# A parallel attention and MLP kernel on one core: x of the second parity and the attention output transposed on VectorE and moved by transfers instead of on TensorE

## The chip, the core and the metric

One core of one Trainium2 chip. The metric is the device time of one execution in microseconds (us); lower is better. The kernel before took 1194.18 us (median of 3 runs, 1194.16 to 1194.31).

## The reference, cut to what matters

```python
x = A_x                                   # 1 x 2048 x 576, float32
xn = _layernorm(x, axis=-1)
return x + _A_ref(xn, A_wqkv, A_wo) + _B_ref(xn, B_w1, B_w2)

def _A_ref(x, wqkv, wo):                  # 32 heads of 18, window 8, dilation 2
    q, k, v = (x @ wqkv) split in three and in heads
    # row s looks at rows s, s-2, ..., s-14; those before row 0 are masked
    o = softmax(q . k_window * 18**-0.5) @ v_window
    return o @ wo

def _B_ref(x, w1, w2):                    # Dff = 4608
    return relu(x @ w1) @ w2
```

## The kernel before, in words

**Tiles and parities.** Because the dilation is 2, even rows attend only to even rows and odd rows to odd rows. The kernel handles one parity ("phase", `ph`) after the other. A phase has 1024 rows, as eight tiles `X[ph, i]` of 128 partitions by 576 columns; partition p of tile i holds row 8p + i of its parity, so a window of 8 rows lies along the free axis.

**Split products.** Each float32 operand is cut into a rounded part (`hi`, float32r) and a rest (`lo`), and a product is made of three terms: hi.hi, lo.hi and hi.lo. The 576 rows of the contraction are four blocks of 128 and a remainder of 64; the fifth block holds the remainder twice, as hi in partitions 0 to 63 and as lo in 64 to 127 (`mix`). `TERMS` lists the 14 matmuls of one product.

**Transposes.** TensorE contracts over partitions, so the normalised x (`xn`) and the attention output must be turned, columns into partitions. `transpose_split` (L264) does this with five TensorE transposes of 128x128 into PSUM (L273, L274). ScalarE then copies `hi` out of PSUM (L276) and `mix` (L278), and VectorE makes `lo` (L277) and the second half of `mix` (L279). `make_xt` (L283) does it for x; two tiles share one `xT` buffer of 256 columns. `wo_a` (L407) does it for the attention output, and `wo_b` (L416) multiplies with `wo` in 28 matmuls of 288 columns and adds the result to `X`. `norm` (L252) copies the last 64 columns once more beside themselves (L261), and `wo_a` does the same into `od` (L411), for the doubled fifth block.

**The steps.** The main loop (L547) runs over 288 steps, 144 per phase: 12 chunks of three 128-wide slices of Dff, by four blocks `tb` of 256 rows, by the three slices. Step n issues `h_mm` of step n + 2 (14 matmuls of 256 columns, the first product of the MLP), then whatever `at` put at this step, then `o_mm` of step n (12 matmuls of 288 columns), then what `late` put there, then VectorE work of the attention from a list (`run_bg`). `h_mm` ends with a ScalarE relu (L447, `hhi`) and a VectorE rest (L448, `hlo`); it has two PSUM buffers, and so has `o_mm`, whose sums VectorE adds to `X` after three steps (L471). Nothing is reordered afterwards: each engine executes its instructions in the order in which the Python code emits them, and an instruction that waits holds up all that stands behind it on its engine.

**What stands where.** In each phase, steps 7 to 95 (counted within the phase) hold the projections for q, k, v of four groups of eight heads; steps 123 to 131 hold `wo_a` and `wo_b` of the eight tiles, one tile per step, `wo_a` at the end of step 123 + i and `wo_b` in the step after it. In the first phase, the x tiles of the second parity are prepared from step 129 on, one every two steps: `load_x`, `stats`, `norm` and `make_xt` (L511 to L515). Block tb of the second phase is first needed by `h_mm` in step 142 + 3 tb.

**Transfers.** All loads and stores are issued by SyncE (SP), in order: three per w1 slice, one per w2 slice, five or six per group of wqkv and of wo, one per x tile and per output tile. A load waits for its staging buffer (`stp`, four of them) to be free. In the built program the transfers of SP and ScalarE use eight semaphores in turn, so each transfer also waits until the eighth before it has landed. ScalarE issues the halo copies of k and v (L318), from SBUF to SBUF.

Of the kernel before, what the change touches and what calls it, by code (L numbers as in the profile page):

```python
# [10 lines left out]
F32 = mybir.dt.float32  # L11
F32R = mybir.dt.float32r
AF = mybir.ActivationFunctionType
ALU = mybir.AluOpType
# [3 lines left out]
P = 128  # L18
# [9 lines left out]
EPS = 1e-5  # L28

UNIT0, UNIT_STEP, WO_AT = 7, 27, 8  # L30
HEADW = (-5, -2, -1, 0, 0, 1)

HEAD = (
# [22 lines left out]
def tile_body(ctx: ExitStack, tc: tile.TileContext, x, wqkv, wo, w1, w2, out):  # L56
    nc = tc.nc
    S, D = x.shape
# [5 lines left out]
    KT = 4  # L64
    DR = D - KT * P
    D2 = D // 2
# [4 lines left out]
    ctx.enter_context(tc.manual_schedule())  # L71
    pool = lambda name, bufs, **k: ctx.enter_context(tc.tile_pool(name=name, bufs=bufs, **k))
    consts = pool("consts", 1)
    xp = pool("xp", 12)
    xtp = pool("xtp", NTB)
    qop = pool("qop", 1)
    kp = pool("kp", 1)
# [9 lines left out]
    tmp = pool("tmp", 2)  # L87
# [4 lines left out]
    f32 = lambda ap: ap.bitcast(F32)  # L92
# [18 lines left out]
    def mm(o, l, r, start, stop, n):  # L111
        nc.tensor.matmul(o, l, r, start=start, stop=stop)  # L112
        t["pe"] += n / 2400.0 + 0.002

    def dve(n):
        t["dve"] += (n + 130) / 960.0
# [112 lines left out]
    X, XT, XN, MR = {}, {}, {}, {}  # L229
# [21 lines left out]

    def norm(ph, i, act=False):  # L252
        nm, r = MR.pop((ph, i))
        xn = tmp.tile([P, 640], F32, name="xn")
        if act:
            nc.scalar.activation(xn[:, 0:D], X[ph, i], AF.Identity, bias=nm)  # L256
            nc.scalar.activation(xn[:, 0:D], xn[:, 0:D], AF.Copy, scale=r)  # L257
        else:
            nc.vector.tensor_scalar(xn[:, 0:D], X[ph, i], nm, r, op0=ALU.add, op1=ALU.mult)
            dve(600)  # L260
        nc.scalar.activation(xn[:, D:640], xn[:, KT * P : D], AF.Copy)  # L261
        XN[ph, i] = xn

    def transpose_split(src, last, hi, mix, lo, free=False):  # L264

        if free:
            pa, pb = (ps_o.tile([P, 2, 512], F32, name="po")[:, 0, :] for _ in range(2))
            pa, pb = pa.rearrange("p (k c) -> p k c", k=KT), pb[:, 0:P]
        else:
            pa = ps_m.tile([P, KT, P], F32, name="pm")  # L270
            pb = ps_m.tile([P, P], F32, name="pm")
        for k in range(KT):
            nc.tensor.transpose(pa[:, k, :], src[:, k * P : (k + 1) * P], ident)  # L273
        nc.tensor.transpose(pb, last, ident)  # L274
        t["pe"] += 5 * 0.06
        nc.scalar.activation(hi, pa, AF.Copy)  # L276
        nc.vector.tensor_tensor(lo, pa, f32(hi), op=ALU.subtract)  # L277
        nc.scalar.activation(mix, pb, AF.Copy)  # L278
        nc.vector.tensor_tensor(mix[DR:P], pb[DR:P], f32(mix[DR:P]), op=ALU.subtract)  # L279
        dve(512)  # L280
        dve(128)

    def make_xt(ph, i, free=False):  # L283
        tb, h = divmod(i, 2)
        if h == 0:
            XT[ph, tb] = xtp.tile([P, 9, TBN], F32R, name="xT")
        d = XT[ph, tb][:, :, h * P : (h + 1) * P]
        xn = XN.pop((ph, i))
        transpose_split(xn[:, 0:512], xn[:, 512:640], d[:, 0:4, :], d[:, 4, :], d[:, 5:9, :], free)


    TERMS = [(k, k) for k in range(KT)] + [(5 + k, k) for k in range(KT)] + [(4, 4)] + [(k, 5 + k) for k in range(5)]


    QO, KK, VV = {}, {}, {}
# [109 lines left out]
    OT = {}  # L405

    def wo_a(ph, i):  # L407
        assert (ph, i) in ready, (ph, i, len(bg))
        o = QO[ph][:, i, :]
        od = tmp.tile([P, 2, DR], F32, name="od")  # L410
        nc.scalar.activation(od, o[:, None, KT * P : D].to_broadcast([P, 2, DR]), AF.Copy)  # L411
        d = tmp.tile([P, 9, P], F32R, name="oT", bufs=1)
        transpose_split(o[:, 0:512], od.rearrange("p a b -> p (a b)"), d[:, 0:4, :], d[:, 4, :], d[:, 5:9, :])
        OT[ph, i] = d

    def wo_b(ph, i):  # L416
        d, w = OT.pop((ph, i)), WO[ph]
        po = [ps_m.tile([P, D2], F32, name="pm") for _ in range(2)]
        for j, (a, b) in enumerate(TERMS):
            for h in range(2):  # L420
                mm(po[h], d[:, a, :], w[b][:, h * D2 : (h + 1) * D2], j == 0, j == len(TERMS) - 1, D2)
        for h in range(2):
            acc = X[ph, i][:, h * D2 : (h + 1) * D2]
            nc.vector.tensor_tensor(acc, po[h], acc, op=ALU.add)
            dve(D2)
# [53 lines left out]
    def at(n, f, *a):  # L479
        todo.setdefault(n, []).append((f, a))  # L480
# [3 lines left out]
    def late(n, f, *a):  # L484
        todo_late.setdefault(n, []).append((f, a))

    plan = []
    for ph in range(NPH):
        b = ph * SPP
        for c in range(NCH):  # L490
            for f in range(C):
                s = b + c * SPC + f
                first = ph == c == 0
                plan.append((HEADW[f] if first else s - 5, w1_task, ((ph, c, f), c * C + f)))
                plan.append((HEADW[3 + f] if first else s - 3, w2_task, ((ph, c, f), c * C + f)))
        for u in range(NU):
            s = b + UNIT0 + u * UNIT_STEP
            plan.append((s - 5, wq_tasks, ((ph, u), u)))
            for i in range(NI):
                at(s + i, qkv_tile, ph, u, i)  # L500
            late(s + NI + 1, attention, ph, u)
        s = b + UNIT0 + NU * UNIT_STEP + WO_AT
        plan.append((s - 8, wo_tasks, (ph,)))
        for i in range(NI):
            late(s + i, wo_a, ph, i)
            at(s + i + 1, wo_b, ph, i)
            at(s + i + 1, done, ph, i)
        if ph + 1 < NPH:
            e = b + SPP - SPC
            for i in range(NI):  # L510
                z = e + 3 + 2 * i  # L511
                at(z - 6, load_x, ph + 1, i)
                late(z - 2, stats, ph + 1, i)
                late(z - 1, norm, ph + 1, i)
                at(z + 1, make_xt, ph + 1, i)  # L515
    for step, f, a in sorted(plan, key=lambda z: z[0]):
        if f in (wq_tasks, wo_tasks):
            f([step + k for k in range(5)], *a)
# [13 lines left out]
    held = []  # L532
    run_splits(-5)
    norm(0, 0)
    norm(0, 1)
    stats(0, 2)
    make_xt(0, 0)
    make_xt(0, 1, True)
    for f in held:
        f()  # L540
# [45 lines left out]
```

## Time and profile before

| | before |
|---|---|
| median of 3 runs | 1194.18 us |
| profiled execution: its time | 1194.74 us |
| profiled execution: its span in the trace | 1193.0 us |
| granted TensorE clock, mean | 0.998 |
| VectorE busy | 812.5 us (68% of the span), 1269 instructions |
| ScalarE busy | 310.5 us (26%), 790 instructions |
| GpSimd busy | 40.1 us (3%) |
| transfers | 84883 packets, 75.67 MB; SP's queue 19.7% of 16 DMA engines |

How to read the profile: it shows one execution. PE is TensorE's matmuls and PEld its weight loads, DVE is VectorE, ACT is ScalarE, POOL is GpSimd, SPq and ACTq are the issuing of transfers by SP and ScalarE. L112 is line 112, the helper through which all matmuls go, so groups of it are told apart by their tiles: `ph` for `h_mm`, `po` for `o_mm`, `pm<-wq,xT` for the projections, `pm<-wq,oT` and `pm<-v,oT` for `wo_b`. "128x576 f32 x192 | 143.9, 757" reads: 192 instructions on 128 partitions by 576 columns, 143.9 us in sum, 757 ns in the mean. In a timeline the first number is the start in us from the beginning of the span, the second the duration of the merged group of xN instructions. PE durations overlap, since matmuls are pipelined; the distance from one start to the next is what counts.

### The profile page before, as it was taken

What the parts mean: (1) busy time and instruction counts of PE and PEld (TensorE: products, weight loads), DVE (VectorE), ACT (ScalarE), POOL (GpSimd) and SP (SyncE); (2) the same over time, 40 slices, a digit from 0 to 9 for tenths busy, and PEclk for the clock granted to TensorE, in tenths of its full rate; (3) what the DMA queues carried; (4) which work ended last, traced back from release to release, by engine and by line L of the source; (5) the groups of instructions that cost most, each with busy time, mean ns of one, the idle gap of its engine ahead of it and who ended that gap; (6) DMA issues with size and microseconds to landing.
All of it is one profiled execution on the core that took longest, in us unless ns stands there. A gap on an engine that the chain in (4) does not pass through costs nothing.

```text
span 1193.0 us, 21739 instructions
## 1 busy us (share of the span) xinstructions
PE 1183.8 (99%) x9016; PEld 1172.8 (98%) x9016; DVE 812.5 (68%) x1269; ACT 310.5 (26%) x790; POOL 40.1 (3%) x63
## 2 busy tenths in 40 slices
PE   8999999999999999999999999999999999999998
PEld 7999999999999999999999999999999999999998
DVE  7516875888687578875573278858767875886732
ACT  5422222131222222322233123122221322222210
POOL 2000000010000000000120000000100000000000
PEclk9999999999999999999999999999999999999999
DMA  5312122130321311402242113031302312212002
GB/s 172 84 32 82 42 76 55 38 107 1 98 58 44 86 33 43 114 11 73 91 130 74 46 54 90 22 85 29 86 21 79 83 38 79 63 42 73 21 1 80
DMA packets 84883, 75.67 MB, mean 63 GB/s; under 512 B 6592, under 2 KB 68288, under 8 KB 84784
## 3 DMA queue, kind: packets, MB, share of 16 engines
q1 hardware_dynamic: 82256, 66.08, 19.7%
q10 hardware_dynamic: 2528, 8.20, 2.4%
q8 instruction: 71, 1.16, 0.4%
q14 instruction: 28, 0.23, 0.1%
HBM read 61.34 MB, written 4.72 MB: 55 GB/s over the span
## 4 chain that ended last, share of the span: by engine, by line
PE 98%; DVE 1%; SPq 0%; ACT 0%; DMA 0%; issue 0%; DVEq 0%; ACTq 0%
PE ph L112 39%; PE po L112 38%; PE pm L112 20%; PE pm L273 1%; PE pm L274 0%; DMA st<-in_w 0%; SPq L235 0%; DVE pr L380 0%; DVE pr L373 0%; SPq L157 0%; SPq L162 0%; SPq L161 0%; PE po L273 0%; ACT xn L257 0%; ACT xn L256 0%
## 5 line engine op out<-in xcount | busy, mean ns | idle before, releaser
L112 PE MATMUL ph<-xT,w1t 128*128 128x256 f32 x4032 | 514.2, 279 | 1.3 <-ACT xT L276 0.6
L112 PEld LDWEIGHTS ph<-xT,w1t 128*128 128x128 f32 x4032 | 491.6, 188 | 2.0 <-ACT xT L276 0.8
L112 PE MATMUL po<-w2t,hhi 128*128 128x288 f32 x2304 | 400.5, 296 | 0.4 <-DVE w2t L143 0.3
L112 PEld LDWEIGHTS po<-w2t,hhi 128*128 128x128 f32 x2304 | 337.0, 188 | 2.0 <-DVE w2t L143 0.5
L447 ACT ACTIVATE hhi<-ph 128x256 fp32r<-128x256 f32 x288 | 110.2, 382 | 531.8 <-PE ph L112 512.5
L112 PE MATMUL po<-w2t,hlo 128*128 128x288 f32 x1152 | 244.7, 293 | 0.0
L448 DVE SCALAR_TENSOR_TENSOR hlo<-ph,hhi 128x256 fp32r<-128x256 f32 x288 | 121.7, 423 | 169.1 <-ACT hhi L447 167.8
L471 DVE TENSOR_TENSOR x<-po,x 128x576 f32<-128x576 f32 x192 | 143.9, 757 | 69.8 <-PE po L112 66.3
L112 PE MATMUL pm<-wq,xT 128*128 128x432 f32 x896 | 185.5, 358 | 0.0
L112 PEld LDWEIGHTS po<-w2t,hlo 128*128 128x128 f32 x1152 | 183.7, 188 | 0.0
L112 PEld LDWEIGHTS pm<-wq,xT 128*128 128x128 f32 x896 | 163.8, 188 | 5.6
L343 DVE TENSOR_TENSOR pr<-qo,k 128x1152 f32<-128x1152 f32 x64 | 85.9, 1349 | 0.0
L373 DVE TENSOR_TENSOR pr<-lg,v 128x1152 f32<-128x1152 f32 x64 | 85.0, 1352 | 0.3
L346 DVE TENSOR_REDUCE lg<-pr 128x64 f32<-128x1152 f32 x64 | 85.0, 1343 | 0.0
L143 DVE TENSOR_TENSOR w2t<-st,w2t 128x576 fp32r<-128x576 f32 x72 | 54.3, 755 | 45.0 <-ACT w2t L146 44.7
L380 DVE TENSOR_TENSOR pr<-pr 128x288 f32<-128x288 f32 (+1 forms) x128 | 70.5, 602 | 0.1
L143 DVE TENSOR_TENSOR w1t<-st,w1t 128x640 fp32r<-128x640 f32 x72 | 59.0, 820 | 15.0 <-ACT w1t L146 14.8
L146 ACT ACTIVATE w2t<-st 128x576 fp32r<-128x576 f32 x72 | 49.1, 684 | 45.0 <-PE po L112 31.0
L146 ACT ACTIVATE w1t<-st 128x640 fp32r<-128x640 f32 x72 | 53.0, 737 | 13.2 <-DMA st<-in_w 13.2
L312 ACT ACTIVATE k<-pm 128x144 f32<-128x144 f32 x64 | 18.7, 292 | 142.8 <-PE pm L112 142.6
L112 PE MATMUL pm<-wq,oT 128*128 128x288 f32 x352 | 51.7, 299 | 0.0
L112 PEld LDWEIGHTS pm<-wq,oT 128*128 128x128 f32 x352 | 47.9, 188 | 1.7
(63 smaller groups left out, 398.0 us busy)
## 6 DMA issues: line engine op xcount, KB each, us to landing
st<-in_w SPq DMA_DIRECT2D x72, 288.0 KB, 3.0
st<-in_w SPq DMA_DIRECT2D x72, 256.0 KB, 3.0
st<-in_wqkv SPq DMA_DIRECT2D x32, 216.0 KB, 3.0
st<-in_w SPq DMA_DIRECT2D x144, 32.0 KB, 2.7
out<-x SPq DMA_DIRECT2D x16, 288.0 KB, 2.1
x<-in_x SPq DMA_DIRECT2D x15, 288.0 KB, 3.9
k<-k ACTq DMA_DIRECT2D x8, 441.0 KB, 3.9
v<-v ACTq DMA_DIRECT2D x8, 441.0 KB, 4.6
```

The costliest lines, as they stand in the source:

```text
L112: nc.tensor.matmul(o, l, r, start=start, stop=stop)
L143: nc.vector.tensor_tensor(lo, src, f32(hi), op=ALU.subtract)
L146: nc.scalar.activation(hi, src, AF.Copy)
L273: nc.tensor.transpose(pa[:, k, :], src[:, k * P : (k + 1) * P], ident)
L312: nc.scalar.activation(k[:, W - 1 + i, :], pq[:, 1, :], AF.Copy)
L343: nc.vector.tensor_tensor(pr[i], q, window(k, i), op=ALU.mult)
L346: nc.vector.tensor_reduce(lg[:, i], pr.pop(i).rearrange(heads, d=Dh), axis=AX.X, op=ALU.add)
L373: nc.vector.tensor_tensor(pr[i].rearrange(heads, d=Dh), e, window(v, i).rearrange(heads, d=Dh), op=ALU.mult)
L380: nc.vector.tensor_tensor(o, z[:, 0:n], z[:, n : 2 * n], op=ALU.add)
L447: nc.scalar.activation(hi, pt, AF.Relu)
L448: nc.vector.scalar_tensor_tensor(lo, pt, 0.0, f32(hi), op0=ALU.max, op1=ALU.subtract)
L471: nc.vector.tensor_tensor(acc, PO[k][:, :, 0:D2], acc, op=ALU.add)
```

## The change

The tiles of the first parity are treated as before. For the eight x tiles of the second parity and the sixteen attention-output tiles, the five TensorE transposes go. Instead `blocks` turns each 32x32 block in place with two VectorE transposes (576 columns, and the last 64 once more) into a tile `tr`, and then SP issues 16 transfers from SBUF to SBUF, each of 32 partitions by 5 runs of 32 columns (128 bytes a run, 20 KB in all), which put block (a, b) where block (b, a) belongs. `split` then makes `hi`, `mix` and `lo` from SBUF; for the attention output `lo` overwrites the turned tile.

The plan moves with it. `wo_a` now stands at steps 123 + (0, 1, 3, 4, 6, 7, 9, 10), the split `wo_s` two steps later at the step's end, and `wo_b` three steps later. For x tile i of the second parity, with z = 134 + 2i: from i = 2 on the load is issued in step z - 2, `stats`, `norm` and the turn all stand at the end of step z, and `make_xt` (the split) at the end of step z + 2, ahead of the `stats` of tile i + 1. There are ten buffers for x tiles instead of twelve, so tile i of the second parity, for i from 2 on, takes the buffer of tile i - 2 of the first and waits for its store. `xn` gets three buffers, which the turned attention output shares. The copy of the last 64 columns (L261, L411) goes where `blocks` is used.

```diff
-    xp = pool("xp", 12)
+    xp = pool("xp", 10)
...
+    def blocks(src, dst):
+        tr = tmp.tile([P, 5, P], F32, name="tr")
+        flat = tr.rearrange("p k c -> p (k c)")
+        nc.vector.transpose(flat[:, 0:D], src)
+        nc.vector.transpose(flat[:, D:640], src[:, KT * P : D])
...
+        for a in range(4):
+            rows = slice(32 * a, 32 * a + 32)
+            for b in range(4):
+                nc.sync.dma_start(dst[32 * b : 32 * b + 32, :, rows], tr[rows, :, 32 * b : 32 * b + 32])
+
+    def turn_x(ph, i):
+        xn = XN[ph, i]
+        blocks(xn[:, 0:D], xn.rearrange("p (k c) -> p k c", c=P))
+
+    def split(z, hi, mix, lo):
+        nc.scalar.activation(hi, z[:, 0:KT], AF.Copy)
+        nc.scalar.activation(mix, z[:, KT], AF.Copy)
+        nc.vector.tensor_tensor(lo, z[:, 0:KT], f32(hi), op=ALU.subtract)
+        nc.vector.tensor_tensor(mix[DR:P], z[DR:P, KT], f32(mix[DR:P]), op=ALU.subtract)
...
+        if ph:
+            split(xn.rearrange("p (k c) -> p k c", c=P), d[:, 0:4, :], d[:, 4, :], d[:, 5:9, :])
+            return
         transpose_split(xn[:, 0:512], xn[:, 512:640], d[:, 0:4, :], d[:, 4, :], d[:, 5:9, :], free)
...
-        transpose_split(o[:, 0:512], od.rearrange("p a b -> p (a b)"), d[:, 0:4, :], d[:, 4, :], d[:, 5:9, :])
-        OT[ph, i] = d
+        OT[ph, i] = tmp.tile([P, 5, P], F32R, name="xn", bufs=3)
+        blocks(QO[ph][:, i, :], f32(OT[ph, i]))
+
+    def wo_s(ph, i):
+        z = OT[ph, i]
+        d = tmp.tile([P, 5, P], F32R, name="oT", bufs=1)
+        split(f32(z), d[:, 0:4], d[:, 4], z[:, 0:4])
...
-            late(s + i, wo_a, ph, i)
-            at(s + i + 1, wo_b, ph, i)
+            z = s + WO_STEPS[i]
+            late(z, wo_a, ph, i)
+            late(z + 2, wo_s, ph, i)
+            at(z + 3, wo_b, ph, i)
...
-                z = e + 3 + 2 * i
-                at(z - 6, load_x, ph + 1, i)
-                late(z - 2, stats, ph + 1, i)
-                late(z - 1, norm, ph + 1, i)
-                at(z + 1, make_xt, ph + 1, i)
+                z = e + 2 + 2 * i
+                at(z - 2 if i > 1 else z - 6, load_x, ph + 1, i)
+                late(z - 2 if i < 2 else z, stats, ph + 1, i)
+                late(z - 1 if i < 2 else z, norm, ph + 1, i)
+                late(z if i < 2 else z, turn_x, ph + 1, i)
+                late(z + 2, make_xt, ph + 1, i)
```

More of the change, by code (lines that the diff above doesn't have):

```diff
@@ L30 @@
 UNIT0, UNIT_STEP, WO_AT = 7, 27, 8
+WO_STEPS = (0, 1, 3, 4, 6, 7, 9, 10)
 HEADW = (-5, -2, -1, 0, 0, 1)
@@ L253, in norm @@
         nm, r = MR.pop((ph, i))
-        xn = tmp.tile([P, 640], F32, name="xn")
+        xn = tmp.tile([P, 640], F32, name="xn", bufs=3)
         if act:
@@ L260, in norm @@
             dve(600)
-        nc.scalar.activation(xn[:, D:640], xn[:, KT * P : D], AF.Copy)
+        if ph == 0:
+            nc.scalar.activation(xn[:, D:640], xn[:, KT * P : D], AF.Copy)
         XN[ph, i] = xn
+    def blocks(src, dst):
[3 more added lines that the diff above has]
+        nc.vector.transpose(flat[:, D:640], src[:, KT * P : D])
+        dve(D)
+        dve(DR)
+        for a in range(4):
[10 more added lines that the diff above has]
+        nc.vector.tensor_tensor(mix[DR:P], z[DR:P, KT], f32(mix[DR:P]), op=ALU.subtract)
+        dve(512)
+        dve(128)
     def transpose_split(src, last, hi, mix, lo, free=False):
@@ L408, in wo_a @@
         assert (ph, i) in ready, (ph, i, len(bg))
[L409 to L412, printed above, removed]
-        transpose_split(o[:, 0:512], od.rearrange("p a b -> p (a b)"), d[:, 0:4, :], d[:, 4, :], d[:, 5:9, :])
-        OT[ph, i] = d
+        OT[ph, i] = tmp.tile([P, 5, P], F32R, name="xn", bufs=3)
[4 more added lines that the diff above has]
+        split(f32(z), d[:, 0:4], d[:, 4], z[:, 0:4])
+        OT[ph, i] = [d[:, k] for k in range(5)] + [z[:, k] for k in range(4)]
     def wo_b(ph, i):
@@ L420, in wo_b @@
             for h in range(2):
-                mm(po[h], d[:, a, :], w[b][:, h * D2 : (h + 1) * D2], j == 0, j == len(TERMS) - 1, D2)
+                mm(po[h], d[a], w[b][:, h * D2 : (h + 1) * D2], j == 0, j == len(TERMS) - 1, D2)
         for h in range(2):
@@ L504, in tile_body @@
         for i in range(NI):
-            late(s + i, wo_a, ph, i)
-            at(s + i + 1, wo_b, ph, i)
-            at(s + i + 1, done, ph, i)
+            z = s + WO_STEPS[i]
+            late(z, wo_a, ph, i)
+            late(z + 2, wo_s, ph, i)
+            at(z + 3, wo_b, ph, i)
+            at(z + 3, done, ph, i)
         if ph + 1 < NPH:
```

## Prediction

> **What bounds the kernel now.** I read the page's busy line and chain first, then PE's timeline for what one step costs, then SP's timeline and the rows of single lines for what one transfer costs.
>
> ```profile
> PE 1183.8 (99%) x9016; PEld 1172.8 (98%) x9016; DVE 812.5 (68%) x1269; ACT 310.5 (26%) x790; POOL 40.1 (3%) x63
> ...
> PE 98%; DVE 1%; SPq 0%; ACT 0%; DMA 0%; issue 0%; DVEq 0%; ACTq 0%
> ```
>
> TensorE bounds everything; nothing waits long ahead of it. So whatever leaves TensorE is gained whole, and whatever delays it is lost whole. PE's timeline around one `wo_b`, and around plain steps later on:
>
> ```profile
> 504.25 0.49 PEld L273 LDWEIGHTS pm<-ident,qo 128*128 128x128 f32 x4
> 504.71 0.14 PEld L274 LDWEIGHTS pm<-ident,od 128*128 128x128 f32 x1
> 504.82 1.68 PEld L112 LDWEIGHTS ph<-xT,w1t 128*128 128x128 f32 x14
> 504.84 1.85 PE L112 MATMUL ph<-xT,w1t 128*128 128x256 f32 x14
> 506.53 3.24 PE L112 MATMUL pm<-wq,oT 128*128 128x288 f32 x22
> 510.40 0.69 PE L112 MATMUL po<-w2t,hhi 128*128 128x288 f32 x4
> 512.45 1.85 PE L112 MATMUL ph<-xT,w1t 128*128 128x256 f32 x14
> ```
> ```profile
> 616.80 1.78 PE L112 MATMUL ph<-xT,w1t 128*128 128x256 f32 x14
> 618.42 0.69 PE L112 MATMUL po<-w2t,hhi 128*128 128x288 f32 x4
> 620.00 1.78 PE L112 MATMUL ph<-xT,w1t 128*128 128x256 f32 x14
> ```
>
> A plain step is 620.00 - 616.80 = 3.2 us: 1.6 for `h_mm`, 1.6 for `o_mm`. A step with `wo_b` and transposes is 512.45 - 504.84 = 7.6; five transposes hold the array from 504.25 to 504.82, 0.57 us; so `wo_b` adds 7.6 - 0.57 - 3.2 = 3.84.
>
> **What goes.** 24 tiles lose five transposes each: 24 x 0.57 = **13.7 us gained** on the bounding engine. The copies of the last 64 columns go from ScalarE, which is idle most of the time: nothing.
>
> **What comes, per tile.** Two VectorE transposes, 16 SP transfers, two ScalarE and two VectorE instructions of the split. The question is how long one tile takes from its turn to its split, and who stands behind it. First the issuing on SP:
>
> ```profile
> 2.11 0.43 SPq L157 DMA_DIRECT2D st<-in_w  x1
> 2.59 0.55 SPq L161 DMA_DIRECT2D st<-in_w  x1
> ...
> 8.42 2.01 SPq L235 DMA_DIRECT2D x<-in_x  x4
> ```
> ```profile
> L173 SPq DMA_DIRECT2D st<-in_w x72: 327/347/530, 10.6 to 1126.4; - x72
> ```
> ```profile
> L161 SPq DMA_DIRECT2D st<-in_w x72: 506/510/1649, 2.6 to 1080.8; - x72
> ```
> ```profile
> L318 ACTq DMA_DIRECT2D v<-v x16: 562/830/834, 91.2 to 1004.4; - x16
> ```
>
> From 2.11 to 8.42 us SP issues eleven transfers in a row, (8.42 - 2.11) / 11 = 0.574 each; L161, which always follows another at once, takes 0.51 and a gap of 0.05 (2.59 - 2.11 - 0.43). No row shows 32 partitions by 5 runs. Below it stands the lone L173, 0.35 + 0.05 = 0.40; above it ScalarE's back-to-back SBUF copies, 0.83 + 0.05 = 0.88. I take **0.575**, the row of a long run on the same queue. Sixteen take 9.2 us, and the last is issued 8.6 after the first. Then the landing, and the data itself:
>
> ```profile
> st<-in_w SPq DMA_DIRECT2D x144, 32.0 KB, 2.7
> out<-x SPq DMA_DIRECT2D x16, 288.0 KB, 2.1
> ...
> v<-v ACTq DMA_DIRECT2D x8, 441.0 KB, 4.6
> ...
> v<-v ACTq DMA_DIRECT2D x8, 59.1 KB, 4.0
> ```
> ```profile
> 656.00:661.00 5.00, 5.00 (x34) 4.90 (x33) 1.73 (x4) 1.04 (x4) 0.00 (x0) 1.00 0.23 66
> ```
>
> I take 2.7 from issue to landing, the nearest size (32 KB; the new ones have 20), between 2.1 and 4.0. So a tile lands 8.6 + 2.7 = 11.3 us after its first issue. The wait for the eighth transfer before costs nothing until landing takes 8 x 0.575 = 4.6. The window holds one w1 slice, 640 packets of 512 bytes and 48 for semaphores: 0.23 x 5 x 16 / 688 = 26.7 ns of one engine each. A tile has 16 x 176 = 2816 packets, at most 2816 x 26.7 ns / 16 = 4.7 us on 16 engines, less than the 9.2 of issuing.
>
> The Trainium skill ("DMA: Bandwidth & Descriptors", Issuing engines are not separate DMA queues) says that the sequencer's time to initiate a transfer is usually small relative to the transfer itself. Under that rule the packets set the pace, which is the third rival below; the L161 row, 0.51 us of issue for 32 KB, speaks against it.
>
> ```profile
> L146 ACT ACTIVATE w2t<-st 128x576 fp32r<-128x576 f32 x72 | 49.1, 684 | 45.0 <-PE po L112 31.0 <-DMA st<-in_w 8.1 <-issue 5.9
> L146 ACT ACTIVATE wq<-st 128x432 fp32r<-128x432 f32 x40 | 22.2, 556 | 2.8 <-DMA st<-in_wqkv 2.8
> L368 DVE TENSOR_TENSOR lg<-lg,r 128x512 f32<-128x512 f32 x8 | 5.5, 690 | 0.2
> L279 DVE TENSOR_TENSOR oT<-pm,oT 64x128 fp32r<-64x128 f32 x16 | 4.7, 295 | 0.5
> L143 DVE TENSOR_TENSOR v<-st,wq 128x576 fp32r<-128x576 f32 x6 | 4.5, 755 | 2.8 <-ACT wq L146 2.8
> L259 DVE TENSOR_SCALAR xn<-x,nm,rstd 128x576 f32<-128x576 f32 x11 | 6.9, 626 | 0.8 <-POOL rstd L248 0.7
> L343 DVE TENSOR_TENSOR pr<-qo,k 128x1152 f32<-128x1152 f32 x64 | 85.9, 1349 | 0.0
> ```
> ```profile
> 612.48 0.81 DVE L243 BATCH_NORM_STATS2 bst<-x 128x6 f32<-128x288 f32 x2
> ```
> ```profile
> 614.30 0.56 POOL L248 TENSOR_TENSOR rstd<-mv,mhalf 128x1 f32<-128x1 f32 x1
> ```
>
> Once landed: `hi` on ScalarE 0.6 (between 0.556 for 432 columns and 0.684 for 576), `lo` and `mix` on VectorE 0.69 + 0.295 = 1.0. The two transposes are shown nowhere: 0.755 (576 columns) + 0.295 = 1.05, the large one bounded by 0.63 and 1.35. `stats` to `rstd` is 612.48 to 614.86, 2.4 us; `norm` 0.6.
>
> **The added wait and what stands behind it.** The split's VectorE instruction waits for a landing, and VectorE takes its work in order. In the attention stage the turn of the next even tile stands right behind the split of an odd one (both at the end of step 126, 129, 132). In the x stage, from tile 2 on, `stats`, `norm` and the turn of tile i + 1 stand right behind the split of tile i. So issue, landing, split and next turn make **one serial chain**. ScalarE's `hhi` and VectorE's `hlo` of later steps stand behind the split too, and with two PSUM buffers for `h_mm`, TensorE can run about two steps ahead and then stops.
>
> *Attention stage, first phase*, from the end of step 123: tile 0 issued at 1.1, tile 1 at 10.3, landed 21.6; + 0.6 + 1.0 + 1.05: tile 2 at 24.2, done 33.4; three w1 transfers ahead of tile 3: 35.1, landed 46.4; tile 4 at 49.1; four transfers between: tile 5 at 60.6, landed 71.9; tile 6 at 74.6, tile 7 at 83.8, landed 95.1. `wo_b` of tile 7 can start at 95.8 and its step ends at 95.8 + 3.84 + 1.6 = 101.2. Without waits, 13 steps and eight `wo_b` end at 41.6 + 30.7 = 72.3: 28.9 late.
>
> *x stage*: after tile 7 (93.0) and two stores, x tile 0 at 94.2, landed 105.5; tile 1 at 108.1, landed 119.4; each further tile 5.65 (0.6 + 1.0 + 2.4 + 0.6 + 1.05) + 11.3 = **17.0 us**, against two steps of 6.4: tile 7 landed at 119.4 + 6 x 17.0 = 221.4, split at 222.1. The `h_mm` that needs it opens step 151, without waits at 72.3 + 14 x 3.2 = 117.1: **105.0 us late**, the 28.9 among them.
>
> *Attention stage, second phase*: the same with fewer loads between: tile 6 at 72.3, tile 7 at 81.5, landed 92.8, step ended 98.9: **26.6 us late**.
>
> Loads of weights and x, and the stores, queue on SP behind the sixteen. Ahead of the next tile SP is free for 17.0 - 9.2 = 7.8 us, and at most seven transfers (4.0) fall there, so they cost nothing; without that cover they cost 0.575 each. Ten x buffers: the load waits for a store issued at least one tile before (landing 2.1 us of a 17.0 us period), nothing.
>
> *Restarts.* At the beginning, after idle time, TensorE was slow:
>
> ```profile
> 11.01 2.62 PE L112 MATMUL ph<-xT,w1t 128*128 128x256 f32 x10 [0.51 <-DVE xT L277]
> 13.42 1.05 PE L273 MATMUL po<-ident,xn 128*128 128x128 f32 x4
> ```
>
> Ten matmuls took 13.42 - 11.01 = 2.4 us, 0.24 each against 1.6 / 14 = 0.115 later. I count 1.7 us for each of the two ends where TensorE takes up again on the path: 3.4; the others lie inside the chain.
>
> **Sum:** 105.0 + 26.6 + 3.4 - 13.7 = +121.3. The profiled execution took 1194.74 (span 1193.0, 1.7 around it), 0.6 above the median: **1316 us**. In series on these chains stand 254 + 127 = 381 issues, so 0.1 us of issue is 38 us of time; 15 landings, -9 to +20 us between the bounds; 15 turns, -2 to +9.
>
> **Rivals.**
> - *Issue at the pace of lone transfers*, 0.40 to 0.45: same chains, 381 x 0.145 = 55 us less at 0.43: 1261 (1250 at 0.40). For it: the new transfers are small. Against: L161 is too, and takes 0.51.
> - *Slower issue*, 0.88 as on ScalarE: 381 x 0.305 = 116 more: 1432. For it: the only SBUF-to-SBUF rows. Against: another queue, and 441 KB in half of them.
> - *Packets set the pace*, 4.7 us a tile, 0.294 a transfer, landed 7.1 after the first issue. TensorE then nearly keeps up in the attention stages (tile 0 ready at 1.1 + 7.1 + 0.65 = 8.8 against 2 x 3.2 + 1.6 = 8.0). x tile 1 is turned after step 136, 72.3 + 0.8 + 1.05 = 74.2; + 7.1 + 6 x (7.1 + 5.65) + 0.7 = 158.5, 41.4 late. 41.4 + 0.8 + 3.4 - 13.7: 1227.
> - *SP's queue alone binds*, VectorE's order holding nothing: 298 issues from the first tile to x tile 7 are 171.4 us, so 58 late, 13 in the second phase: 1256. Against: the order of the code.
> - *Not slower*: the tiles land within the steps given, and only the 13.7 us remain: 1181. It decides where the x period fits in two steps: 8.4 us without any issuing is already over 6.4; were `stats` and `norm` done during the landing, 5.4 + 15 issues would fit below 0.07 us each. No issue in the trace is below 0.33.
>
> That the change does not take the transposes away is excluded by its code.
>
> **Chances.** Forecast, issue 0.50 to 0.65 (1287 to 1345): 0.56. Lone pace 0.17, queue alone 0.08, slower issue 0.09, packets 0.06, not slower 0.04, of which 0.03 faster and 0.01 within 0.2%, which is about what a measurement of this kernel can tell from no change. The range 1240 to 1390 takes in the first three and issue up to 0.77; slower: 0.96.
>
> **What would show it.** SP solid with DMA_DIRECT2D rows of 0.5 to 0.6 us, sixteen together, and some 8 us between x tiles; PE idle some 10 us in 17 through the x stage, its releaser the VectorE or ScalarE split (L286 to L289), theirs a transfer into `xn`; twelve plain steps there some 100 us longer; the projections unchanged. It is wrong if issue times are far from 0.575, if landings grow beyond 4.6, or if VectorE reaches the next turn before the split.

## The result, and the profile after

The changed kernel takes 1340.07 us (median of 4 runs, 1338.91 to 1341.0) against 1194.24 (median of 4): ratio 1.122, 95% interval 1.1201 to 1.1239, **146 us slower**. The forecast was 1316 (1240 to 1390). The profiled execution took 1338.91 us, its span is 1337.1.

From the page of the changed kernel: busy time by engine, the clock granted to TensorE in 40 slices, and the chain that ended last.

```profile
PE 1210.7 (91%) x8896; PEld 1196.9 (90%) x8896; DVE 828.4 (62%) x1317; ACT 305.7 (23%) x766; POOL 38.9 (3%) x63
...
PEclk9999999999999998878776899999999999998889
...
PE 73%; SPq 16%; DVE 4%; DMA 3%; issue 2%; ACT 1%; POOL 0%; ACTq 0%; DVEq 0%; POOLq 0%
```

TensorE is down from 99% to 91% of a longer span, and 16% of the chain is SP issuing, which had 0% before. The clock row shows the two places: the middle, where attention output and x are turned, and the end. The same two by stage: busy time of each engine in stretches, first the kernel before, then the changed one. The cuts are the end of step 123, the start of step 151 (its `h_mm` needs x tile 7), and for the changed kernel also the middle of the stage. The columns are the stretch, its length, busy time and instructions of PE, PEld, DVE, ACT and POOL, the granted TensorE clock, the DMA engines' share and GB/s.

```profile
0.00:504.25 504.25, 499.17 (x3764) 494.09 (x3764) 356.79 (x543) 141.49 (x354) 20.32 (x35) 1.00 0.25 69
504.25:630.71 126.46, 126.38 (x1009) 125.30 (x1008) 82.77 (x169) 35.58 (x92) 9.82 (x18) 1.00 0.25 75
630.71:1193.00 562.29, 558.22 (x4248) 553.42 (x4246) 372.99 (x558) 133.41 (x344) 9.97 (x10) 1.00 0.20 56
```
```profile
0.00:503.38 503.38, 498.98 (x3764) 493.82 (x3765) 356.66 (x544) 141.66 (x353) 20.84 (x35) 1.00 0.24 68
503.38:604.00 100.62, 77.65 (x511) 76.27 (x510) 47.84 (x100) 13.55 (x32) 1.50 (x4) 0.85 0.24 51
604.00:740.37 136.37, 66.73 (x420) 64.75 (x418) 45.00 (x100) 17.79 (x44) 6.56 (x14) 0.74 0.28 69
740.37:1337.10 596.73, 567.37 (x4206) 562.08 (x4206) 378.92 (x575) 132.67 (x338) 9.97 (x10) 0.97 0.22 58
```

Up to step 123 the kernels are alike. Steps 124 to 150 took 126.5 us and now take 100.6 + 136.4 = 237.0: 110.5 longer, where the forecast had 105.0 - 16 x 0.57 = 95.9. The rest took 562.3 and takes 596.7: 34.4 longer. TensorE's timelines, the kernel before and then the changed one, show where step 267 ends, after which the second phase's attention output is turned:

```profile
1092.65 0.60 PE L273 MATMUL pm<-ident,qo 128*128 128x128 f32 x4
```
```profile
1204.05 1.78 PE L113 MATMUL ph<-xT,w1t 128*128 128x256 f32 x14
```

Up to there the rest took 1092.65 - 630.71 = 461.9 and takes 1204.05 - 740.37 = 463.7, a restart's 1.7 more; from there to the end 100.4 and now 133.0, 32.7 more, where the forecast had 26.6 - 4.6 = 22.0. In the x stage TensorE is busy for half of the time, at a mean clock of 0.74. DMA engines are at 0.28: they do not set the pace.

One link of the x stage in the changed kernel's timeline (start, duration; in brackets how long the engine was idle before, and what ended that): tile 5 is issued, lands and is split, and tile 6 is prepared and issued.

```profile
691.77 10.57 SPq L278 DMA_DIRECT2D xn<-tr  x16
...
704.31 0.63 ACT L286 ACTIVATE xT<-xn 128x512 fp32r<-128x512 f32 x1 [15.93 <-DMA xn<-tr]
...
704.97 0.69 DVE L288 TENSOR_TENSOR xT<-xn,xT 128x512 fp32r<-128x512 f32 x1 [10.74 <-ACT xT L286]
704.99 3.36 PE L113 MATMUL ph<-xT,w1t 128*128 128x256 f32 x14 [7.54 <-ACT xT L286]
...
706.01 0.82 DVE L244 BATCH_NORM_STATS2 bst<-x 128x6 f32<-128x288 f32 x2
...
707.42 0.57 POOL L249 TENSOR_TENSOR rstd<-mv,mhalf 128x1 f32<-128x1 f32 x1
708.02 0.58 DVE L260 TENSOR_SCALAR xn<-x,nm,rstd 128x576 f32<-128x576 f32 x1 [0.76 <-POOL rstd L249]
...
708.64 0.78 DVE L271 STREAM_TRANSPOSE tr<-xn 128x576 f32<-128x576 f32 x1
...
709.57 10.98 SPq L278 DMA_DIRECT2D xn<-tr  x16
```

This is the chain of the prediction. ScalarE waited 15.93 us for the landing, VectorE 10.74 for ScalarE, TensorE 7.54; from the split's start to the next first issue are 709.57 - 704.31 = 5.3 us, and 12.5 from first issue to split. What single transfers and transposes cost (minimum, median, maximum in ns), and the landing, counted from the start of the issue:

```profile
L278 SPq DMA_DIRECT2D xn<-tr x384: 585/602/1564, 503.9 to 1303.3; - x192
...
DMA to landing us min/median/max: 1.8/1.9/3.7
```
```profile
L271 DVE STREAM_TRANSPOSE tr<-xn x8: 778/778/779, 598.0 to 726.8; 128x576 f32<-128x576 f32 x8
```
```profile
L272 DVE STREAM_TRANSPOSE tr<-xn x8: 202/202/204, 598.8 to 727.5; 128x64 f32<-128x64 f32 x8
```

First issues, in us from the end of step 123, as forecast and as in the trace (less 503.38):

| | attention tile 3 | 4 | 5 | 6 | x tile 0 | 1 | step 151 |
|---|---|---|---|---|---|---|---|
| forecast | 35.1 | 49.1 | 60.6 | 74.6 | 94.2 | 108.1 | 222.1 |
| trace | 38.2 | 52.7 | 66.0 | 81.3 | 103.8 | 118.5 | 237.0 |

The rows behind the x tiles, of SP's timeline in the changed kernel, with x tile 7 as the last:

```profile
607.22 10.58 SPq L278 DMA_DIRECT2D xn<-tr  x16
...
621.83 11.25 SPq L278 DMA_DIRECT2D xn<-tr  x16
...
727.77 10.37 SPq L278 DMA_DIRECT2D xn<-tr  x16
```

Six periods took 727.77 - 621.83 = 105.94, 17.66 us each (forecast 17.0).

### The profile page after: what moved, and what is told of

It is laid out like the page before. It is cut to its first block, busy times and chain, and to the rows that moved or that the text cites. A ratio compares the mean times of both kernels' runs of the same rounds, so it can differ in the third digit from the quotient of the medians.

```text
span 1337.1 us, 22162 instructions
## 1 busy us (share of the span) xinstructions
PE 1210.7 (91%) x8896; PEld 1196.9 (90%) x8896; DVE 828.4 (62%) x1317; ACT 305.7 (23%) x766; POOL 38.9 (3%) x63
## 4 chain that ended last, share of the span: by engine, by line
PE 73%; SPq 16%; DVE 4%; DMA 3%; issue 2%; ACT 1%; POOL 0%; ACTq 0%; DVEq 0%; POOLq 0%
PE ph L113 30%; PE po L113 29%; SPq L278 15%; PE pm L113 14%; DMA xn<-tr 2%; DVE bst L244 1%; DVE tr L271 1%; ACT oT L286 1%; DVE xn L288 0%; DVE xn L260 0%; ACT xT L286 0%; DVE pr L412 0%; POOL rstd L249 0%; DVE w2t L144 0%; DVE xT L288 0%
## 5 line engine op out<-in xcount | busy, mean ns | idle before, releaser
L113 PE MATMUL ph<-xT,w1t 128*128 128x256 f32 x4032 | 521.2, 281 | 40.7 <-DVE hlo L482 23.1
L113 PEld LDWEIGHTS ph<-xT,w1t 128*128 128x128 f32 x4032 | 499.2, 191 | 42.8 <-DVE hlo L482 23.8
L113 PE MATMUL po<-w2t,hhi 128*128 128x288 f32 x2304 | 404.8, 298 | 29.5 <-DVE x L505 28.9
L113 PEld LDWEIGHTS po<-w2t,hhi 128*128 128x128 f32 x2304 | 341.5, 191 | 31.5 <-issue 29.4
L113 PEld LDWEIGHTS pm<-wq,oT 128*128 128x128 f32 x224 | 43.4, 258 | 53.8 <-ACT oT L286 53.8
L147 ACT ACTIVATE w2t<-st 128x576 fp32r<-128x576 f32 x72 | 49.1, 684 | 59.2 <-PE po L113 42.3
L288 DVE TENSOR_TENSOR xn<-xn,oT 128x512 fp32r<-128x512 f32 x16 | 11.1, 692 | 71.8 <-ACT oT L286 69.0
```

The costliest lines, as they stand in the source:

```text
L147: nc.scalar.activation(hi, src, AF.Copy)
```

## The experiments

Theory A is the prediction's chain, with the trace's issue pace of 0.66 us. Its main rival, theory B, is that SP's queue alone holds everything. Where no number of runs is given, there was one; the kernel before, run beside them, took 1193.8 to 1196.3.

**1 and 2. One half of the change alone.** In the first, `wo_a`, `wo_b` and their steps are those of before. In the second, x goes back to TensorE:

```diff
-                late(z if i < 2 else z, turn_x, ph + 1, i)
-                late(z + 2, make_xt, ph + 1, i)
+                at(z + 2, make_xt, ph + 1, i)      # with transpose_split
```

> Only the x tiles of the second parity go over VectorE and transfers; the attention output is turned on TensorE at the steps of the kernel before. Theory A (one serial chain of issue, landing, split and next turn, with the issue pace of the changed kernel, 0.66 us a transfer): x tile 0 is issued 72 us after the end of step 123, tile 1 at 87, each further tile 17.6 later, tile 7 split at 205, against 122 without waits: 84 us late, 1.7 restart, 4.6 saved: 1275 us, and the distance between x tiles stays 17 to 18 us. Theory B (SP's queue alone holds the x stage, VectorE's order nothing): 152 issues in a row are 100 us, 52 late: 1243 us.

Measured: 1273.92 us, beside 1194.35 for the kernel before. Theory A holds, in the distance too: x tile 1 is issued at 590.99 us and tile 7 at 695.62, 17.4 a tile.

> Only the attention output goes over VectorE and transfers; the x tiles are turned on TensorE, at the steps and with the loads and buffers of the changed kernel. Theory A (serial chain): 37 us late in the first phase and 36 in the second, two restarts 3.4, 9.1 saved: 1261 us; the x stage as fast as before. Theory B (SP's queue alone): 24 us late in each phase: 1236 us. Either way a time far above 1261 would mean that the ten x buffers and the later loads cost something by themselves.

Measured: 1266.13. Nearer to theory A, which is 5 us short. Ten x buffers and later loads are in this kernel too, so they cost little by themselves. The halves add 79.6 and 71.8 us, 151 together, about the whole.

**3. The order on VectorE.** The same instructions; at a step that has both, the turn stands ahead of the split.

```diff
-                late(z + 2, make_xt, ph + 1, i)
+            for i in range(NI):                    # after all turns
+                late(e + 4 + 2 * i, make_xt, ph + 1, i)
```

(and `wo_s` likewise)

> The changed kernel with one difference in order: where a turn (with its stats and norm) and the split of the tile before stand at the end of the same step, the turn is emitted first, so VectorE does not wait for a landing ahead of it. Theory A (VectorE's order makes the chain): SP now runs without pauses, 298 issues of 0.66 us up to x tile 7, 83 us late, and 24 in the second phase: about 1290 us, x tiles 12 to 13 us apart. Theory B (VectorE's order holds nothing): 1340 us and x tiles 17 to 18 us apart, as now.

Measured: 1294.8, 45 us less than the changed kernel. Its VectorE timeline has the transposes first, and the wait behind them; SP's has x tiles 1 and 7:

```profile
659.39 0.78 DVE L271 STREAM_TRANSPOSE tr<-xn 128x576 f32<-128x576 f32 x1
660.09 0.20 DVE L272 STREAM_TRANSPOSE tr<-xn 128x64 f32<-128x64 f32 x1
666.04 0.69 DVE L288 TENSOR_TENSOR xT<-xn,xT 128x512 fp32r<-128x512 f32 x1 [5.75 <-ACT xT L286]
```
```profile
611.83 11.27 SPq L278 DMA_DIRECT2D xn<-tr  x16
...
692.78 10.38 SPq L278 DMA_DIRECT2D xn<-tr  x16
```

The period is (692.78 - 611.83) / 6 = 13.5 us instead of 17.66. So the order of turn and split on VectorE was worth 45 us. What is left is SP's queue: from the first turned tile's issues to those of x tile 7, SP's pauses of more than 0.3 us are 1.0 us in all, against 38.8 in the changed kernel.

**4. The same number of transfers, a fifth of the bytes** (x tiles only): `dst[..., 0:1, rows]` from `tr[rows, 0:1, ...]`, one run of the five. The other blocks stay where they are, and here and in experiment 5 GpSimd fills the last 64 columns with zeros.

> The changed kernel with the sixteen transfers of each x tile of the second parity cut to one of five runs, 4 KB instead of 20 (four blocks in five stay where they were, so the second parity is computed from wrongly turned x). Theory A (the issuing on SP sets the pace, not the data): 1340 us within 5, a transfer still 0.66 us apart from the next. Theory C (packets or bytes set the pace): the sixteen take a fifth, x tiles come some 8 us closer together: about 1280 us.

Measured: 1335.22, theory A. Sixteen transfers of 4 KB take SP as long as sixteen of 20 (tiles 6 and 7):

```profile
707.07 10.86 SPq L280 DMA_DIRECT2D xn<-tr  x16
724.94 10.05 SPq L280 DMA_DIRECT2D xn<-tr  x16
```

**5. Half the number** (x tiles only): `for b in range(2)`, those into partitions 0 to 63.

> The changed kernel with eight of the sixteen transfers of each x tile of the second parity, those into partitions 0 to 63 (the other half of each tile stays where it was, so the second parity is computed from wrongly turned x). Theory A (the number of issues in series sets the time): eight tiles lose 8 x 0.66 us each, 42 us less: 1298 us, x tiles 12 to 13 us apart. Theory D (what is left between tiles, landing and the work of VectorE and ScalarE, sets it): 1335 to 1340 us.

Measured: 1300.26, theory A. Tiles 1 and 7:

```profile
619.05 5.96 SPq L280 DMA_DIRECT2D xn<-tr  x8
...
693.35 5.25 SPq L280 DMA_DIRECT2D xn<-tr  x8
```

12.4 us a tile, 5.3 less than 17.66: eight issues of 0.66. Experiment 4 leaves the count and cuts the bytes, this one halves both: the count of issues costs, the bytes do not.

**6. Two queues.**

```diff
-                nc.sync.dma_start(dst[32 * b ...
+                (nc.sync if a < 2 else nc.scalar).dma_start(dst[32 * b ...
```

> The changed kernel with eight of the sixteen transfers of every tile issued by ScalarE, the other eight by SP. Theory A (each queue has its own issue pace): SP's part is 5.3 us, ScalarE's eight at 0.6 to 0.88 are 5 to 7, so each of 15 links in series loses 4 to 5 us: about 1275 us. Theory E (what issues is shared by the queues, so that each transfer takes twice as long when both run): about 1340 us, single issues near 1.2 us. Slower than 1340 would mean that ScalarE's own work waits behind its issues.

Measured: 1291.92, between the theories' numbers. The single issues decide against E; what ScalarE waited for (us in all, times, longest) shows where A's other 17 us may have gone:

```profile
L278 ACTq DMA_DIRECT2D xn<-tr x192: 592/614/1727, 504.0 to 1250.5; - x192
L278 SPq DMA_DIRECT2D xn<-tr x192: 585/607/2112, 504.1 to 1250.9; - x192
```
```profile
ACT hhi L481 <- DMA xn<-tr: 90.5, 11, 10.8
ACT w2t L147 <- DMA xn<-tr: 52.7, 6, 11.3
```

Each queue issues at its own 0.61, but ScalarE's relu and weight copies now stand behind its issues. That this is the whole difference was not tried. The Trainium skill (Perfetto Trace Analysis, DMA Optimizations) says that where descriptor generation is the bottleneck, spreading transfers over the engines that can issue them may help: 48 us less here agree.

**7. Another shape** (x tiles only): sixteen transfers of 128 partitions by 40 columns.

```diff
+                    c = slice(160 * a + 40 * b, 160 * a + 40 * b + 40)
+                    nc.sync.dma_start(wide[:, c], flat[:, c])
```

> The changed kernel, but the sixteen transfers of each x tile of the second parity have another shape: 128 partitions by one run of 40 columns, from the same columns to the same columns, again 20 KB (so the blocks stay where they are, and the second parity is computed from wrongly turned x). In the changed kernel sixteen transfers take 10.3 to 11.4 us on SP, 0.60 each and a gap of 0.05, where the prediction took 0.575. Theory G (the shape of 32 partitions by five runs makes an issue dear; a full-width one goes at the pace of the full-width loads that follow one another, 0.50 to 0.57): 8 x 15 issues are 10 to 18 us cheaper, 1322 to 1330 us. Theory H (any transfer that follows another at once on SP costs about 0.6): sixteen still take over 10 us, 1335 to 1340 us.

Measured: 1327.4, which is G's number, but not for G's reason. SP's timeline, tiles 1 and 7:

```profile
621.63 11.19 SPq L280 DMA_DIRECT2D xn<-tr  x16
...
717.96 10.19 SPq L280 DMA_DIRECT2D xn<-tr  x16
```

The period is (717.96 - 621.63) / 6 = 16.1 us instead of 17.66. The sixteen still take over 10, as H has it: from tile 1 to 6 11.19 + 10.13 + 10.16 + 10.79 + 10.29 + 10.89 = 63.45, 10.6 each, against 64.7 / 6 = 10.8 in the changed kernel. What got shorter is the pause from the last issue to the next tile, 5.5 instead of 6.9. With transfers by columns, `hi` needs only the first thirteen, and the trace agrees: in each x tile `hi` starts 0.07 to 0.30 us after the thirteenth has landed and 1.6 to 1.8 us ahead of the landing of the last. In the changed kernel it starts after the last has landed.

**8 and 9. A version after these findings.** x stays on TensorE, with its preparation moved by some steps. The attention output is turned in pairs of tiles, so that sixteen transfers, with ten runs instead of five, serve two tiles. Turn and split stand five steps apart for the first two pairs in 8 and for the first in 9, otherwise four.

```diff
+TURN, SPLIT = (1, 4, 8, 11), (6, 9, 12, 15)      # 8
+TURN, SPLIT = (1, 6, 9, 12), (6, 10, 13, 16)     # 9
...
+        both = [tmp.tile([P, 2, 640], d, name="xn", bufs=3) for d in (F32, F32R)]
+        tr, z = (f32(t).rearrange("p h (k c) -> p (h k) c", c=P) for t in both)
...
+            if h == 0:
+                late(s + TURN[p], turn, ph, p)
+            late(s + SPLIT[p] + h, wo_s, ph, i)
+            at(s + SPLIT[p] + h + 1, wo_b, ph, i)
```

> Another version: x is turned on TensorE as in the kernel before, the attention output in pairs of tiles: four VectorE transposes, then sixteen transfers with ten runs each instead of five. The turns stand at steps 124, 127, 131 and 134, the splits five steps later (four for the last), so no turn stands behind a split it need not wait for. Theory A (issue count and order set the time): sixteen issues are 10.6 us a pair, and a pair has 16 us or more until its split; 16 x 0.57 = 9.1 us less than the kernel before: 1185 us. Theory F (weights and x loads queued behind sixteen issues come late, or transfers of twice the bytes take longer to issue): at or above 1194 us.

Measured: 1202.24 (4 runs), before 1194.46: ratio 1.0062 (1.0045 to 1.0078). Theory A missed by 17 us, and theory F holds in its first half: 10.8 of the 17 are two waits of TensorE, and the other 6 are not assigned. The two, and the stretch of one of them:

```profile
PE pm L114 <- ACT w2t L148: 10.8, 2, 5.8
```
```profile
520.77 10.81 SPq L282 DMA_DIRECT2D xn<-xn  x16
...
531.68 1.02 SPq L175 DMA_DIRECT2D st<-in_w  x2
...
535.33 0.68 ACT L148 ACTIVATE w2t<-st 128x576 fp32r<-128x576 f32 x1 [9.71 <-DMA st<-in_w]
...
536.18 0.62 ACT L286 ACTIVATE oT<-xn 128x512 fp32r<-128x512 f32 x1
```

A w2 load that was due waits behind sixteen issues; ScalarE waits 9.71 us for it, and the split, whose data had long landed, stands behind it on ScalarE.

> The version with pairs again, with other steps: the turns at 124, 129, 132 and 135 instead of 124, 127, 131 and 134, the splits at 129, 133, 136 and 139, the x tiles' norm one step later each where it must. In the pairs version TensorE lost 10.8 us to two waits of the attention product behind a ScalarE split of a w2 slice, whose load was issued behind the sixteen transfers of the second pair; with the second turn at the end of step 129 the loads due in steps 129 to 131 are issued ahead of it. Theory A (issue count and order set the time): those waits go, with the slow restarts after them; 9.1 us less than the kernel before: 1185 to 1188 us. Theory F (something else in the pairs version costs time, such as transfers of twice the bytes): 1192 us or more.

Measured: **1187.06** (5 runs, 1186.47 to 1188.4), before 1195.18: ratio 0.9931 (0.9917 to 0.9945), 8 us faster than the kernel before. TensorE is busy throughout, the w2 loads (L175) now stand ahead of the second sixteen, and the issues are as long as ever:

```profile
PE 1171.8 (99%) x8936; PEld 1162.2 (98%) x8936; DVE 821.4 (69%) x1301; ACT 307.8 (26%) x774; POOL 41.9 (4%) x63
```
```profile
508.59 10.62 SPq L282 DMA_DIRECT2D xn<-xn  x16
...
521.17 1.00 SPq L175 DMA_DIRECT2D st<-in_w  x2
...
529.26 10.88 SPq L282 DMA_DIRECT2D xn<-xn  x16
```

## Why the prediction was right

- *TensorE bounds, and five transposes are worth 0.57 us.* Experiment 9 bears it out: sixteen tiles should give 9.1 us and gave 8.1.
- *One serial chain of issue, landing, split and next turn.* Shown by experiment 3, which changes only the order (-45 us), and by the link above.
- *Issues set the chain, not packets.* Shown by 4 and 5. The row that spoke against the packet rival, L161, was read rightly. The rule of the Trainium skill (DMA: Bandwidth & Descriptors, Issuing engines are not separate DMA queues) that the sequencer's time is usually small relative to the transfer does not hold for these: one issue takes 0.60 us and one landing 1.9, and sixteen issues in series take 10.6.
- *The mis-sized term is the issue of one transfer.* Taken as 0.575, it was 0.60 with a gap of 0.05, and in nine of the 24 sets of sixteen one issue took 0.89 to 1.56; the eight x tiles take (10.58 + 11.25 + 10.28 + 10.38 + 11.24 + 10.57 + 10.98 + 10.37) / 128 = 0.669. Over the 381 issues in series that is 36 us more. Experiment 7 leaves the pace where it was, so the shape that it changes is not the cause.
- *Landing* was 1.9 instead of 2.7: 15 x 0.8 = 12 us less. The two transposes took 0.98 instead of 1.05, and `stats` to `rstd` 707.99 - 706.01 = 2.0 instead of 2.4: some 4 us less. 1316 + 36 - 12 - 4 = 1336, against 1338.9 for the profiled execution. Between landing and split lay another 0.07 to 0.61 us, 3.9 over the 15, which the sum put at nothing; that is about what is left.
- *What was luck.* A pace of 0.669 lies just outside the 0.50 to 0.65 of the forecast's main case, and with nothing else off it gives 1316 + 36 = 1352, above that case's 1287 to 1345. The shorter landing brought the time back inside. The chain, its order and what releases whom were not luck.
- *Restarts.* After 7.54 us of idling 14 matmuls took 3.36 us instead of 1.78: 1.6 a restart, where 1.7 was taken.
- *Rivals.* SP's queue alone was priced at 1256 with the old pace; at 0.66 the same sum gives 1290, and experiment 3 gave 1294.8. It was a true limit, behind the chain. Lone-transfer pace and ScalarE's 0.88 were both off: SP issues these in 0.60, and ScalarE in 0.61.
- *Loads behind the sixteen cost nothing.* Right for this kernel, where SP pauses between tiles and TensorE waits for weights for 1.6 us in all; wrong in experiment 8, where a load that was due stood behind them.

For the mis-sized term, the trace of the kernel before held a nearer row than the mean of 0.574: L162, which follows L161 and is of the same 32 KB.

```profile
L162 SPq DMA_DIRECT2D st<-in_w x72: 583/589/1158, 3.2 to 1081.3; - x72
```

Its median with the gap is 0.64, while the mean has L157's 0.43 in it. Why one load takes 0.43 and another 0.59 stays open.

## What to carry to other kernels

Count issues, not bytes: many small transfers cost their number times the pace of one queue, so let each carry more (two tiles in one set of sixteen) before adding queues. When an instruction that waits for a transfer is put on an in-order engine, look at what stands right behind it: if that is what starts the next transfer, latency and issue add up tile by tile. And a block of issues must not stand ahead of a load that falls due before the block is through.

## What the runs showed of the hardware that was not expected

- SP needs 0.59 to 0.61 us for a transfer from SBUF to SBUF with 4, 20 or 40 KB (sixteen: 10.0 to 11.8 us), and issuing from SP and ScalarE at once leaves both at 0.61.
- A VectorE transpose of 128x576 float32 takes 0.77 us, about as long as an elementwise operation of two inputs of that size (0.755).
